# New lists of jobs for the front and the attention of a retention, MLP and attention kernel; two chunks' scores in wider blocks; the last chunk's keys left in HBM

## The chip, the cores and the metric

One core of a Trainium2 chip runs the kernel. The metric is the device time of one execution in microseconds, as the median of repeated runs. Engines are named as the profile names them: PE multiplies matrices (PEld is its loading of weights), DVE, ACT and POOL work on elements, and SP issues most of the DMA transfers.

## The reference

Three layers on 2 batches of 768 positions, all in fp32:

```python
# retention, 8 heads of 64, blocks of 64 positions
intra = einsum(einsum(qb, kb) * Dmask, vb)          # Dmask[i, j] = lam ** (i - j) for i >= j
out   = intra + einsum(qb * lam_pow, kv_state)
kv_state = lam ** block * kv_state + einsum(kb * rev_pow, vb)
# layer norm and MLP, 512 -> 2048 -> 512
x = x + relu(layer_norm(x) * g_ln @ w_ch1) @ w_ch2
# four experts, each a causal softmax attention with 64 columns; the two best by x @ w_gate are mixed
```

## The kernel before

**Retention.** Each batch is cut into 6 chunks of 128 positions, 12 in all. For chunk n, `load_qk` brings queries and keys with the head's columns on the partitions, and `load_kv` keys and values with the positions on the partitions; each is one transfer of 512 KB. Then, with the letters of the list: `S` scores on PE into PSUM (`ret_scores`), `A` their decay on DVE, `Ka` and `Kg` the keys' scaling for the state (three heads on ACT, five on POOL), `Q` the queries' scaling on POOL, `T` the chunk's state on PE, `D` the running state on DVE, `O` its decay on POOL, `U` queries by state on PE, `I` decayed scores by values on PE, on top of `U`, and `C` three copies of the result out of PSUM on ACT. The last chunk of a batch, numbers 5 and 11, needs no `T`, and so no `Ka` or `Kg`. `S` and `U` with `I` write tiles of two PSUM banks, of which there are two ("big"); four tiles of one bank ("mid") serve the others.

**Layer norm and MLP.** Three chunks make a block of 384 positions. `ma`, `mc`, `mm`, `mi` are the sums, their copy on ACT, the mean on PE and its subtraction on DVE; `sq`, `va`, `vc`, `vd` do the same for the variance; `xs` and `lo` split the block into two parts in fp32r. A weight piece comes as raw words and is unpacked by `z` and `h` on ACT and `l`, `t`, `r`, `e`, `p` on DVE. `P` is one MLP step on PE, twelve matmuls of 384 columns, and `LA`, `LD` are its ReLU on ACT and DVE. 

**Order of the front.** All engines work through one list written out by hand, `FRONT`. Every token is issued in that order on its engine, and each engine takes its own instructions in order. `k`, `q` and `w` issue the loads of kv, qk and weights on the SP queue, `G` the load of the norm's gain on ACT's queue, `W` three warm-up matmuls. Two tokens of different engines that wait for nothing of each other are free against each other.

**Attention.** After the MLP, projections of a block of positions are 8 jobs (`f` takes the next: three of values, the gate, four of queries and keys). Rows of 128 queries with an expert each are items 0 to 47, in the order of `ROWS`. `s` are scores on PE with mask, maximum and exponential behind them, `c` the weighting on POOL, `t` the transposes on PE, `v` weights by values, `o` the output. `ORDER` sets PE's order and the order in which the other engines' work is written; for those the scheduler chooses. The weights before their transpose have 7 buffers, those after it 8.

Of the kernel before, what the change touches and what calls it, by code (L numbers as in the profile page):

```python
# [71 lines left out]

# [3 lines left out]


FRONT = """
    Ka:0 S:0 Kg:0 k:1 S:1 T:0 q:2 A:0 Ka:1 G D:0 A:1 I:0 k:2 W w Kg:1 q:3 O:0 T:1 S:2 C:0 Q:1 D:1 q:4 Q:2 U:1 Ka:2
    w z:0 k:3 I:1 Kg:2 k:4 S:3 O:1 A:2 Q:4 l:0 t:0 q:5 U:2 T:2 C:1 I:2 A:3 h:0 Q:3 q:6 k:5 D:2 S:4 Kg:3 q:7 C:2  # L80
    O:2 Ka:3 A:4 U:3 r:0 T:3 e:0 Kg:4 D:3 z:1 I:3 k:6 C:3 l:1 O:3 w Ka:4 ma:0 q:8 p:0 S:5 mc:0 k:7 Ka:6 U:4 mm:0
    I:4 A:5 T:4 Kg:6 Q:5 D:4 C:4 mi:0:0 sq:0:0 S:6 A:6 T:6 Q:7 U:5 mi:0:1 t:1 xs:0:0 I:5 D:6 xs:0:1 O:6 S:7 I:6
    C:5 xs:0:2 k:8 Kg:7 w lo:0:1 sq:0:1 k:9 Ka:7 va:0 C:6 ma:1 A:7 q:9 T:7 xs:0:3 lo:0:0 S:8 lo:0:2 Kg:8 Q:8
    Ka:8 U:7 D:7 Kg:9 O:7 h:1 lo:0:3 k:10 I:7 A:8 mc:1 r:1 T:8 C:7 Kg:10 q:10 mm:1 mi:1:0 mi:1:1 P:g1:0:0:0 S:9
    Ka:9 xs:1:0 Ka:10 e:1 U:8 D:8 LA:g1:0:0:0 xs:1:1 xs:1:2 I:8 C:8 T:9 q:11 vc:0 sq:1:0 A:9 k:11 w Q:9 O:8
    sq:1:1 Q:11 lo:1:2 z:2 S:10 lo:1:1 lo:1:0 vd:0 A:10 U:9 Q:10 D:9 p:1 I:9 xs:1:3 lo:1:3 va:1 C:9 ma:2 l:2
    S:11 O:9 t:2 U:10 LD:g1:0:0:0 vc:1 I:10 T:10 mc:2 vd:1 mm:2 h:2 P:g1:0:1:0 r:2 D:10 C:10 mi:2:0 P:g1:0:0:1
    xs:2:0 U:11 e:2 mi:2:1 xs:2:1 A:11 LA:g1:0:1:0 lo:2:0 w sq:2:0 LD:g1:0:1:0 xs:2:2 I:11 xs:2:3 sq:2:1 lo:2:3
    P:g1:0:1:1 LA:g1:0:0:1 p:2 LD:g1:0:0:1 C:11 park:0 LA:g1:0:1:1 z:3 va:2 lo:2:2 LD:g1:0:1:1 park:1 ma:3 l:3
    t:3 P:g1:0:0:2 lo:2:1 z:4 X mc:3 LA:g1:0:0:2 h:3 vc:2 r:3 mm:3 mi:3:0 e:3 mi:3:1 xs:3:0 p:3 P:g1:0:1:2  # L90
    xs:3:1 LD:g1:0:0:2 LA:g1:0:1:2 xs:3:2 z:5 LD:g1:0:1:2 P:g1:0:2:0 l:4 P:g1:0:2:1 w LA:g1:0:2:0 l:5 P:g1:0:2:2
    lo:3:2 t:4 sq:3:1 P:g1:0:0:3 lo:3:1 LD:g1:0:2:0 LA:g1:0:2:1 h:4 r:4 P:g1:0:1:3 LA:g1:0:2:2 LD:g1:0:2:1
    sq:3:0 LA:g1:0:0:3 xs:3:3 park:2 park:3 t:5 LD:g1:0:2:2 va:3 vc:3 h:5 P:g1:0:2:3 e:4 lo:3:3 p:4 P:g2f:0:0:0
    w LD:g1:0:0:3 LA:g1:0:1:3 z:6 lo:3:0 r:5 LA:g1:0:2:3 LD:g1:0:1:3 P:g1:0:3:0 w l:6 e:5 p:5 P:g2f:0:0:1 t:6 w
    h:6 LD:g1:0:2:3 z:7 r:6 P:g1:0:3:1 l:7 LA:g1:0:3:0 e:6 LA:g1:0:3:1 vd:3 LD:g1:0:3:0 w p:6 vd:2 t:7 h:7
    LD:g1:0:3:1 r:7 e:7 p:7
"""


# [950 lines left out]
```

## Time and profile before

| what | value |
|---|---|
| median of 3 runs | 457.24 us (457.09 to 457.62) |
| the profiled execution | 457.37 us, its span 455.6 us |
| granted TensorE clock | 1.00 in every stage |
| busy share of the span: PE, DVE, ACT, POOL | 98%, 73%, 46%, 18% |
| front, attention | 0 to 98 us, 322.4 to 455.6 us |

The span runs from the first to the last instruction. The profiled execution's own time is longer by what lies around its instructions. Ends of matmuls are modelled, so PE counts as busy over short waits; the distance between starts tells them.

### The profile page before, as it was taken

How to read it: one execution, taken by the hardware profiler on the slowest of the kernel's cores; microseconds unless marked ns; L12 is line 12 of the kernel's file. 1: busy time of each engine (PE TensorE's matmuls, PEld its weight loads, DVE VectorE, ACT ScalarE, POOL GpSimd, SP SyncE). 2: the span in 40 equal slices, each digit the busy share in tenths (PEclk: the TensorE clock that was granted, in tenths of full speed). 3: DMA queues.
4: the chain of work that ended last, by engine and by line, in shares of the span. 5: the costliest groups of instructions: out<-in, count | busy, mean ns of one | idle time of the engine just before them, and what ended most of it. 6: DMA issues, size and time to landing. Idle time of an engine off the chain costs nothing.

```text
span 455.6 us, 9079 instructions
## 1 busy us (share of the span) xinstructions
PE 447.5 (98%) x3563; PEld 421.5 (93%) x3563; DVE 331.9 (73%) x698; ACT 208.9 (46%) x476; POOL 83.2 (18%) x132
## 2 busy tenths in 40 slices
...
GB/s 295 393 371 288 137 83 199 93 51 157 122 92 75 65 94 85 54 0 48 90 96 108 182 48 74 36 88 1 0 1 0 25 25 23 24 2 48 24 47 71
DMA packets 15226, 42.33 MB, mean 93 GB/s; under 512 B 2240, under 2 KB 5072, under 8 KB 15184
## 3 DMA queue, kind: packets, MB, share of 16 engines
...
q8 instruction: 28, 0.46, 0.4%
q10 hardware_dynamic: 288, 0.13, 0.1%
...
## 4 chain that ended last, share of the span: by engine, by line
PE 94%; DMA 3%; ACT 1%; issue 0%; POOL 0%; DVE 0%; SPq 0%
PE h L553 29%; PE y L589 27%; PE pj L815 7%; PE s L895 5%; PE av L945 5%; PE t L933 4%; PE pv L837 4%; PE o L966 4%; DMA early<-in_qkT 2%; PE po L431 2%; PE yf L611 2%; PE sc L367 2%; PE ps L412 1%; PE po L422 1%; DMA qk<-in_qkT 1%; PE va L471 1%
## 5 line engine op out<-in xcount | busy, mean ns | idle before, releaser
L553 PE MATMUL h<-xn,w 128*128 128x384 f32 x768 | 139.6, 336 | 0.0
L553 PEld LDWEIGHTS h<-xn,w 128*128 128x128 f32 x768 | 133.5, 188 | 2.2 <-DVE hs L575 0.6
L589 PE MATMUL y<-hs,w 128*128 128x384 f32 x552 | 99.7, 334 | 0.0
L589 PEld LDWEIGHTS y<-hs,w 128*128 128x128 f32 x552 | 96.1, 188 | 0.0
L572 ACT ACTIVATE hs<-h 128x384 fp32r<-128x384 f32 x50 | 24.5, 491 | 114.2 <-PE h L553 104.7
L829 POOL TENSOR_SCALAR kh<-kh 64x384 fp32r<-64x384 f32 x16 | 8.1, 507 | 295.4 <-ACT kh L826 293.4
L575 DVE SCALAR_TENSOR_TENSOR hs<-h,hs 128x384 fp32r<-128x384 f32 x50 | 27.7, 555 | 34.1 <-ACT hs L572 34.1
L923 POOL TENSOR_SCALAR att<-att,c,gw 128x128 f32<-128x128 f32 (+5 forms) x48 | 34.7, 730 | 46.0 <-DVE c L920 24.4
L597 DVE TENSOR_TENSOR xT<-xT,y 128x768 f32<-128x768 f32 x24 | 22.8, 952 | 27.3 <-PE y L589 27.3
L815 PE MATMUL pj<-x,wa 128*128 128x384 f32 x192 | 36.0, 340 | 0.0
L277 ACT CAST w<-top 128x512 fp32r<-128x512 f32 x32 | 19.8, 620 | 30.0 <-DVE top L269 30.0
L815 PEld LDWEIGHTS pj<-x,wa 128*128 128x128 f32 x192 | 33.1, 188 | 0.3 <-issue 0.2
L934 ACT COPY aT<-t 128x512 f32<-128x512 f32 (+3 forms) x64 | 26.4, 442 | 9.2 <-PE t L933 9.0
L933 PE MATMUL t<-ident,att 128*128 128x128 f32 x168 | 26.1, 275 | 0.0
L933 PEld LDWEIGHTS t<-ident,att 128*128 128x128 f32 x168 | 20.1, 140 | 3.1 <-issue 1.2
L895 PE MATMUL s<-kh,qs 128*128 128x384 f32 (+4 forms) x64 | 22.8, 362 | 0.0
L260 ACT ACTIVATE mag<-raw 128x512 f32<-128x512 f32 x31 | 20.4, 670 | 4.6 <-DVE w L288 2.1
L288 DVE TENSOR_TENSOR w<-top,mag 128x512 fp32r<-128x512 f32 x32 | 22.0, 688 | 0.3
L285 DVE TENSOR_TENSOR top<-top,w 128x512 f32<-128x512 f32 x32 | 21.9, 684 | 0.0
L282 DVE SCALAR_TENSOR_TENSOR mag<-raw,mag 128x512 f32<-128x512 uint32 x31 | 21.4, 689 | 0.7
L269 DVE SCALAR_TENSOR_TENSOR top<-raw,mag 128x512 int32<-128x512 int32 x31 | 21.4, 689 | 0.6
L945 PE MATMUL av<-aT,v 128*64 128x128 f32 x336 | 21.5, 277 | 0.0
...
## 6 DMA issues: line engine op xcount, KB each, us to landing
...
```

Of the source, the lines that this page charges most:

```text
L288: nc.vector.tensor_tensor(t["w"][:, 1], t["top"], t["mag"], ALU.add)
L553: nc.tensor.matmul(ph[:, :TB], w[:, wi, k, :], xn[:, xi, k, :], start=(i == 0), stop=(i == 11))
L572: LAST.append([nc.scalar.activation(h[:, 0], ph[:, :TB], AF.Relu)])
L575: LAST[-1].append(nc.vector.scalar_tensor_tensor(h[:, 1], ph[:, :TB], 0.0, h[:, 0].bitcast(F32), ALU.max, ALU.subtract))
L589: nc.tensor.matmul(y[:, j, :TB], w[:, wi, e * P:(e + 1) * P], h[:, xi], start=(f == 0 and i == 0), stop=(f == GF - 1 and i == 2))
L597: nc.vector.tensor_tensor(xv, xv, y[:, :, :TB], ALU.add)
L815: nc.tensor.matmul(ps[:, :TB], w[:, wi, k, :], x2[:, xi, k, :], start=(i == 0), stop=(i == 11))
L895: nc.tensor.matmul(ps[:, c], q, kk[:, e, c * m:(c + 1) * m], start=(i == 0), stop=(i == 1))
L923: nc.gpsimd.tensor_scalar(a[:, :n], a[:, :n], c, gw, ALU.mult, ALU.mult)
L933: nc.tensor.transpose(pt[:, (j - j0) * P:(j - j0 + 1) * P], a[:, j * P:(j + 1) * P], ident)
L934: nc.scalar.copy(aT[:, j0 * P:j1 * P], pt[:, :(j1 - j0) * P])
L945: nc.tensor.matmul(pav[e2 * HD:(e2 + 1) * HD, pr * P:(pr + 1) * P], v[:, j, e * HD:(e + 1) * HD], row["aT"][e][:, j * P:(j + 1) * P], star ...
```

## The change

`FRONT` and `ORDER` hold the same tokens in another order. In `ret_scores` the first two chunks take one matmul per head with 128 stationary columns instead of two with 64. For the last chunk of a batch `load_kv` brings the values alone.

```diff
+WHOLE = 2
 ORDER = """
-    s0 s1 f f s2 s3 c0 s4 c1 c2 s5 c3 f s6 c4 s7 t0 t1 f c5 f t2 c6 f t3 s8 c7 s9 t4 c8 s10 v1 v3 t5 c9 c10 f t6
...
-    f s19 t13 f t14 f f o11 c18 f t15 s20 c19 s21 t16 s22 c20 t17 v13 v15 s23 t18 s24 f o15 s25 c21 t19 c22 c23
...
-    s31 s32 t27 o23 t28 s33 c30 t29 s34 c31 c32 s35 v25 v27 c33 c34 c35 t30 s36 c36 o27 t31 s37 c37 t32 s38 v29
...
-    t41 s46 v37 v39 c45 t42 c46 s47 t43 v41 v43 t44 t45 o39 c47 t46 t47 v45 v47 o43 o47
+    s0 s1 c0 c1 s4 f s5 f f c5 s2 s3 c4 f s6 c3 c6 s7 t1 t4 f s8 f s9 f t0 c7 f c9 s10 s11 f t7 s12 f t3 t5 f v1 t8
+    t2 s16 c2 c11 s13 v3 v5 t6 o3 c13 v7 t10 f s17 t11 s18 f s19 f s14 c19 t9 f c18 c17 s15 f c12 c15 f s20 s21 t17
+    t13 f v9 v11 t19 t18 c16 c14 s24 f s22 f t14 c20 s23 c10 c23 f f t16 f c21 c8 t12 t15 s25 o11 s26 c24 f t22 s28
+    v13 v15 v17 s27 t23 t20 s29 t21 o15 s30 c25 v21 v19 t25 s31 c27 s32 t27 s33 c26 c29 o19 c22 t29 c28 c31 s34 t28
+    s35 s36 v23 t24 o7 s37 t26 c33 c35 t34 v25 s38 t31 s40 c36 t32 c30 v29 v27 s41 t36 c38 s42 t35 c41 t30 s43 t33
+    o23 s39 v31 v33 v35 t38 c43 o31 t40 c37 o27 t37 t41 s44 c39 t39 s45 c44 v41 v37 c34 v39 c45 t42 s46 s47 t44 c32
+    c47 c42 t43 c46 t45 o39 o35 t46 t47 v43 v45 c40 v47 o43 o47
 """
 FRONT = """
-    Ka:0 S:0 Kg:0 k:1 S:1 T:0 q:2 A:0 Ka:1 G D:0 A:1 I:0 k:2 W w Kg:1 q:3 O:0 T:1 S:2 C:0 Q:1 D:1 q:4 Q:2 U:1 Ka:2
-    w z:0 k:3 I:1 Kg:2 k:4 S:3 O:1 A:2 Q:4 l:0 t:0 q:5 U:2 T:2 C:1 I:2 A:3 h:0 Q:3 q:6 k:5 D:2 S:4 Kg:3 q:7 C:2
-    O:2 Ka:3 A:4 U:3 r:0 T:3 e:0 Kg:4 D:3 z:1 I:3 k:6 C:3 l:1 O:3 w Ka:4 ma:0 q:8 p:0 S:5 mc:0 k:7 Ka:6 U:4 mm:0
-    I:4 A:5 T:4 Kg:6 Q:5 D:4 C:4 mi:0:0 sq:0:0 S:6 A:6 T:6 Q:7 U:5 mi:0:1 t:1 xs:0:0 I:5 D:6 xs:0:1 O:6 S:7 I:6
...
-    sq:1:1 Q:11 lo:1:2 z:2 S:10 lo:1:1 lo:1:0 vd:0 A:10 U:9 Q:10 D:9 p:1 I:9 xs:1:3 lo:1:3 va:1 C:9 ma:2 l:2
-    S:11 O:9 t:2 U:10 LD:g1:0:0:0 vc:1 I:10 T:10 mc:2 vd:1 mm:2 h:2 P:g1:0:1:0 r:2 D:10 C:10 mi:2:0 P:g1:0:0:1
...
+    k:1 Kg:0 Ka:0 S:0 A:0 G W Q:1 k:2 Kg:1 q:2 S:1 Kg:2 T:0 D:0 O:0 I:0 Ka:1 U:1 q:3 Q:2 q:4 T:1 Ka:2 T:2 A:1 I:1
+    S:2 D:1 O:1 D:2 w k:3 C:0 w k:4 S:3 U:2 Q:4 Q:3 q:5 A:2 I:2 k:5 S:4 Kg:3 C:1 O:2 C:2 ma:0 k:6 q:6 A:3 z:0 Ka:3
+    q:7 l:0 T:3 D:3 t:0 O:3 Kg:4 Kg:6 mc:0 Ka:4 h:0 A:4 q:8 r:0 z:1 U:3 I:3 mm:0 T:4 l:1 S:5 k:7 U:4 A:5 mi:0:0 Q:5
+    I:4 Q:7 D:4 t:1 C:3 C:4 k:8 Ka:6 S:6 A:6 U:5 I:5 q:9 q:10 T:6 e:0 sq:0:0 k:9 S:7 mi:0:1 xs:0:0 D:6 I:6 C:5 ma:1
...
+    xs:1:1 A:9 T:9 xs:1:2 sq:1:0 C:8 sq:1:1 lo:1:2 e:1 p:1 O:8 k:11 Q:9 q:11 Q:11 P:g1:0:0:0 LA:g1:0:0:0 z:2 vc:0
+    vd:0 lo:1:1 lo:1:0 xs:1:3 S:10 D:9 O:9 U:9 I:9 z:3 A:10 ma:2 Ka:10 lo:1:3 va:1 mc:2 l:2 mm:2 mi:2:0 C:9 vc:1
+    T:10 Q:10 xs:2:0 mi:2:1 xs:2:1 D:10 l:3 t:2 h:2 LD:g1:0:0:0 r:2 U:10 S:11 t:3 vd:1 A:11 I:10 C:10 P:g1:0:1:0
...
 """
@@ def load_kv
-        nc.sync.dma_start(kvn, kv[b, c])
+        if c < NC - 1:
+            nc.sync.dma_start(kvn, kv[b, c])
+        else:
+            nc.sync.dma_start(kvn[:, 1], kv[b, c, :, 1])
@@ def ret_scores
         for hp, h2 in HEADS:
+            if n < WHOLE:
+                nc.tensor.matmul(sc[:, h2, cols(hp)], r["qk"][half(h2), 1, hp, :], r["qk"][half(h2), 0, hp, :],
+                                 start=True, stop=True, skip_group_check=True)
+                continue
             for kh in range(2):
```

## Rows read from the trace of the kernel before

**Rows 1.** The page: busy time, share of the span and instructions of each engine.
```profile
PE 447.5 (98%) x3563; PEld 421.5 (93%) x3563; DVE 331.9 (73%) x698; ACT 208.9 (46%) x476; POOL 83.2 (18%) x132
```
**Rows 2.** Windows: stretch, busy PE, PEld, DVE, ACT, POOL; clock; DMA share, GB/s.
```profile
16.20:28.00 11.80, 11.15 (x252) 8.64 (x252) 7.98 (x11) 5.50 (x17) 5.56 (x7) 1.00 1.02 408
28.00:39.50 11.50, 11.26 (x245) 8.54 (x243) 10.57 (x15) 10.49 (x29) 8.95 (x10) 1.00 0.97 358
39.50:57.20 17.70, 17.70 (x284) 14.80 (x282) 16.14 (x26) 14.73 (x34) 6.11 (x6) 1.00 0.48 165
...
98.00:322.40 224.40, 224.40 (x1296) 224.40 (x1295) 158.66 (x272) 68.05 (x120) 0.00 (x0) 1.00 0.25 77
322.40:455.60 133.20, 129.91 (x1047) 119.64 (x1046) 97.67 (x301) 82.50 (x223) 51.76 (x80) 1.00 0.07 25
```
**Rows 3.** The chain that ended last: start, us, what.
```profile
28.06 1.03 PE sc L367 x32
...
45.02 1.03 PE sc L367 x32
...
57.22 0.60 PE po L422 x16
...
65.48 12.48 PE h L553 x72
```
**Rows 4.** Timeline of PE from 16 us: start, us, instruction, count, idle before.
```profile
16.21 1.10 PE L367 MATMUL sc<-early 64*64 64x128 f32 x32 [2.01 <-DMA early<-in_qkT]
17.11 0.65 PE L422 MATMUL po<-qd,st 64*64 64x128 f32 x16
17.68 0.69 PE L412 MATMUL ps<-kvn,kd 128*64 128x64 f32 x16
18.20 1.05 PE L431 MATMUL po<-a,kvn 128*64 128x128 f32 x16
19.17 1.10 PE L367 MATMUL sc<-qk 64*64 64x128 f32 x32
```
**Rows 5.** Groups by line and shape, 5 to 57 us: busy us, mean ns; idle before.
```profile
L398 DVE TENSOR_TENSOR a<-sc,dec 128x1024 f32<-128x1024 f32 x12 | 14.6, 1220 | 4.1 <-PE sc L367 4.1
...
L457 ACT COPY xT<-po 64x256 f32<-64x256 f32 x22 | 8.1, 367 | 0.3
...
L392 POOL TENSOR_TENSOR kd<-kvn,dec 128x320 f32<-128x320 f32 x8 | 6.7, 836 | 5.5 <-PE po L431 2.9 <-DVE a L398 1.1 <-PE ps L412 1.0
...
L441 DVE TENSOR_TENSOR st<-ps,old 128x256 f32<-128x256 f32 x8 | 3.4, 419 | 2.8 <-PE ps L412 2.8
...
L392 POOL TENSOR_TENSOR kd<-early,dec 128x320 f32<-128x320 f32 x2 | 1.5, 730 | 0.0
```
**Rows 6.** Timeline of ACT and its queue, 9 to 14 us.
```profile
9.19 0.38 ACTq L688 DMA_DIRECT2D g_sb<-in_g_ln  x1
...
11.81 0.83 ACT L386 ACTIVATE kd<-kvn,dec 128x64 f32<-128x64 f32 x3 [0.29 <-DMA kvn<-in_kv]
13.13 0.71 ACT L260 ACTIVATE mag<-raw 128x512 f32<-128x512 f32 x1 [0.49 <-DMA raw<-in_w]
```
**Rows 7.** Timeline of all engines around 381 us.
```profile
380.25 0.47 ACT L826 CAST kh<-pj 64x384 fp32r<-64x384 f32 x1 [1.58 <-PE pj L815]
...
381.65 0.42 PE L895 MATMUL s<-kh,qs 128*128 128x384 f32 x1
...
382.24 0.44 PE L895 MATMUL s<-kl,qs 128*128 128x384 f32 x1 [0.17 <-POOL kl L829]
```
**Rows 8.** Timeline of PE from 444 us.
```profile
444.68 1.97 PE L945 MATMUL av<-aT,v 128*64 128x128 f32 x32
...
448.56 0.92 PE L945 MATMUL av<-aT,v 128*64 128x128 f32 x8
449.40 3.07 PE L966 MATMUL o<-wa,avs 128*128 128x512 f32 x18
```
**Rows 9.** The page: costliest groups, out<-in count, busy us, mean ns, idle before.
```profile
L934 ACT COPY aT<-t 128x512 f32<-128x512 f32 (+3 forms) x64 | 26.4, 442 | 9.2 <-PE t L933 9.0
```

More of the change, by code (lines that the diff above doesn't have):

```diff
@@ L62 @@
 ORDER = """
-    s0 s1 f f s2 s3 c0 s4 c1 c2 s5 c3 f s6 c4 s7 t0 t1 f c5 f t2 c6 f t3 s8 c7 s9 t4 c8 s10 v1 v3 t5 c9 c10 f t6
-    f s11 s12 t7 s13 f t8 c11 o3 f t9 s14 t10 c12 s15 v5 c13 v7 s16 c14 f t11 s17 c15 c16 t12 c17 s18 o7 v9 v11
-    f s19 t13 f t14 f f o11 c18 f t15 s20 c19 s21 t16 s22 c20 t17 v13 v15 s23 t18 s24 f o15 s25 c21 t19 c22 c23
-    s26 t20 c24 f f t21 c25 c26 s27 t22 f c27 f t23 f v17 v19 f f s28 s29 t24 c28 o19 c29 t25 s30 v21 v23 t26
-    s31 s32 t27 o23 t28 s33 c30 t29 s34 c31 c32 s35 v25 v27 c33 c34 c35 t30 s36 c36 o27 t31 s37 c37 t32 s38 v29
-    c38 v31 t33 s39 t34 s40 t35 s41 t36 o31 c39 c40 v33 c41 s42 t37 s43 t38 v35 c42 t39 s44 c43 o35 t40 s45 c44
-    t41 s46 v37 v39 c45 t42 c46 s47 t43 v41 v43 t44 t45 o39 c47 t46 t47 v45 v47 o43 o47
+    s0 s1 c0 c1 s4 f s5 f f c5 s2 s3 c4 f s6 c3 c6 s7 t1 t4 f s8 f s9 f t0 c7 f c9 s10 s11 f t7 s12 f t3 t5 f v1 t8
[5 more added lines that the diff above has]
+    c47 c42 t43 c46 t45 o39 o35 t46 t47 v43 v45 c40 v47 o43 o47
 """
@@ L78 @@
 FRONT = """
-    Ka:0 S:0 Kg:0 k:1 S:1 T:0 q:2 A:0 Ka:1 G D:0 A:1 I:0 k:2 W w Kg:1 q:3 O:0 T:1 S:2 C:0 Q:1 D:1 q:4 Q:2 U:1 Ka:2
-    w z:0 k:3 I:1 Kg:2 k:4 S:3 O:1 A:2 Q:4 l:0 t:0 q:5 U:2 T:2 C:1 I:2 A:3 h:0 Q:3 q:6 k:5 D:2 S:4 Kg:3 q:7 C:2
-    O:2 Ka:3 A:4 U:3 r:0 T:3 e:0 Kg:4 D:3 z:1 I:3 k:6 C:3 l:1 O:3 w Ka:4 ma:0 q:8 p:0 S:5 mc:0 k:7 Ka:6 U:4 mm:0
-    I:4 A:5 T:4 Kg:6 Q:5 D:4 C:4 mi:0:0 sq:0:0 S:6 A:6 T:6 Q:7 U:5 mi:0:1 t:1 xs:0:0 I:5 D:6 xs:0:1 O:6 S:7 I:6
-    C:5 xs:0:2 k:8 Kg:7 w lo:0:1 sq:0:1 k:9 Ka:7 va:0 C:6 ma:1 A:7 q:9 T:7 xs:0:3 lo:0:0 S:8 lo:0:2 Kg:8 Q:8
@@ L84 @@
-    Ka:8 U:7 D:7 Kg:9 O:7 h:1 lo:0:3 k:10 I:7 A:8 mc:1 r:1 T:8 C:7 Kg:10 q:10 mm:1 mi:1:0 mi:1:1 P:g1:0:0:0 S:9
-    Ka:9 xs:1:0 Ka:10 e:1 U:8 D:8 LA:g1:0:0:0 xs:1:1 xs:1:2 I:8 C:8 T:9 q:11 vc:0 sq:1:0 A:9 k:11 w Q:9 O:8
-    sq:1:1 Q:11 lo:1:2 z:2 S:10 lo:1:1 lo:1:0 vd:0 A:10 U:9 Q:10 D:9 p:1 I:9 xs:1:3 lo:1:3 va:1 C:9 ma:2 l:2
-    S:11 O:9 t:2 U:10 LD:g1:0:0:0 vc:1 I:10 T:10 mc:2 vd:1 mm:2 h:2 P:g1:0:1:0 r:2 D:10 C:10 mi:2:0 P:g1:0:0:1
-    xs:2:0 U:11 e:2 mi:2:1 xs:2:1 A:11 LA:g1:0:1:0 lo:2:0 w sq:2:0 LD:g1:0:1:0 xs:2:2 I:11 xs:2:3 sq:2:1 lo:2:3
@@ L89 @@
[L89 to L93, printed above, removed]
@@ L94 @@
-    w LD:g1:0:0:3 LA:g1:0:1:3 z:6 lo:3:0 r:5 LA:g1:0:2:3 LD:g1:0:1:3 P:g1:0:3:0 w l:6 e:5 p:5 P:g2f:0:0:1 t:6 w
-    h:6 LD:g1:0:2:3 z:7 r:6 P:g1:0:3:1 l:7 LA:g1:0:3:0 e:6 LA:g1:0:3:1 vd:3 LD:g1:0:3:0 w p:6 vd:2 t:7 h:7
-    LD:g1:0:3:1 r:7 e:7 p:7
+    k:1 Kg:0 Ka:0 S:0 A:0 G W Q:1 k:2 Kg:1 q:2 S:1 Kg:2 T:0 D:0 O:0 I:0 Ka:1 U:1 q:3 Q:2 q:4 T:1 Ka:2 T:2 A:1 I:1
+    S:2 D:1 O:1 D:2 w k:3 C:0 w k:4 S:3 U:2 Q:4 Q:3 q:5 A:2 I:2 k:5 S:4 Kg:3 C:1 O:2 C:2 ma:0 k:6 q:6 A:3 z:0 Ka:3
+    q:7 l:0 T:3 D:3 t:0 O:3 Kg:4 Kg:6 mc:0 Ka:4 h:0 A:4 q:8 r:0 z:1 U:3 I:3 mm:0 T:4 l:1 S:5 k:7 U:4 A:5 mi:0:0 Q:5
@@ new lines @@
+    I:4 Q:7 D:4 t:1 C:3 C:4 k:8 Ka:6 S:6 A:6 U:5 I:5 q:9 q:10 T:6 e:0 sq:0:0 k:9 S:7 mi:0:1 xs:0:0 D:6 I:6 C:5 ma:1
+    xs:0:1 Q:8 xs:0:2 O:6 lo:0:1 sq:0:1 va:0 mc:1 Ka:7 w Kg:7 T:7 p:0 A:7 C:6 k:10 xs:0:3 lo:0:0 lo:0:2 Kg:8 Kg:9
+    lo:0:3 mm:1 mi:1:0 S:8 A:8 Ka:8 U:7 D:7 T:8 I:7 C:7 h:1 O:7 Ka:9 r:1 w w D:8 Kg:10 S:9 U:8 I:8 mi:1:1 xs:1:0
+    xs:1:1 A:9 T:9 xs:1:2 sq:1:0 C:8 sq:1:1 lo:1:2 e:1 p:1 O:8 k:11 Q:9 q:11 Q:11 P:g1:0:0:0 LA:g1:0:0:0 z:2 vc:0
+    vd:0 lo:1:1 lo:1:0 xs:1:3 S:10 D:9 O:9 U:9 I:9 z:3 A:10 ma:2 Ka:10 lo:1:3 va:1 mc:2 l:2 mm:2 mi:2:0 C:9 vc:1
@@ new lines @@
+    T:10 Q:10 xs:2:0 mi:2:1 xs:2:1 D:10 l:3 t:2 h:2 LD:g1:0:0:0 r:2 U:10 S:11 t:3 vd:1 A:11 I:10 C:10 P:g1:0:1:0
+    P:g1:0:0:1 LA:g1:0:1:0 lo:2:0 U:11 h:3 LA:g1:0:0:1 r:3 sq:2:0 xs:2:2 xs:2:3 e:2 I:11 sq:2:1 LD:g1:0:1:0 lo:2:3
+    P:g1:0:1:1 LD:g1:0:0:1 p:2 park:0 C:11 e:3 z:4 LA:g1:0:1:1 p:3 LD:g1:0:1:1 va:2 lo:2:2 lo:2:1 l:4 ma:3
+    P:g1:0:0:2 w park:1 X mc:3 mm:3 P:g1:0:1:2 LA:g1:0:0:2 w mi:3:0 mi:3:1 xs:3:0 xs:3:1 LA:g1:0:1:2 vc:2 P:g1:0:2:0
+    LA:g1:0:2:0 LD:g1:0:0:2 P:g1:0:2:1 t:4 h:4 xs:3:2 z:5 P:g1:0:2:2 P:g1:0:0:3 LA:g1:0:2:1 LA:g1:0:2:2 lo:3:2
```

4 lines of the change are left out of this document (added).

## The prediction

> **What bounds the kernel now.** I read the page's engine line first, then the granted clock and the busy times stage by stage, then the chain of waits, then the timeline of single engines where the chain is not plain PE work. PE is busy 98% of the span [rows 1], so only time in which PE has nothing to do, or waits with a matmul still in its pipe, can be won; the work itself is the same in both versions but for two chunks' scores. The stages [rows 2] say where to look: the clock is 1.00 everywhere; from 98 to 322.4 us PE and its weight loads fill the stage completely and neither list touches the order there. What is left is the front (up to 98 us) and the attention (322.4 us on).
>
> A "busy" PE hides waits, because the modelled end of a matmul covers short ones. So I price a job by the distance between starts [rows 4]: a chunk's scores S 0.90 (16.21 to 17.11), its outer part U 0.57 (to 17.68), its state T 0.52 (to 18.20), its inner part I 0.97 (to 19.17). A layer-norm sum I put at 0.7 and a mean at 0.4 (estimates, from the I and the twelve matmuls of an MLP step, which take 2.08: 12.48 for 72 from 65.48 on [rows 3]).
>
> Front: from the first S at 5.50 to S6 (scores of chunk 6, 28.06 in the chain [rows 3]) PE does 6 S, 5 T, 4 U, 5 I, one sum, one mean and the second warm-up: about 17.0 us of work in 22.6, so 5.5 idle. The largest piece is S3, which waits 2.01 us for its query/key load [rows 4]. Loads come every 1.3 us: two that follow each other release ACT at 11.81 and 13.13 [rows 6]; but the next one comes only at 16.2, 3.1 us later. What the trace has beside them is the gain vector's load, issued at 9.19 [rows 6], in elements of four bytes. I put the missing 1.8 us (3.1 less 1.3) on it. After 28 us loads are no longer last: DVE is busy 10.57 and ACT 10.49 of 11.50, then 16.14 and 14.73 of 17.70 [rows 2]. There PE follows the decay products on DVE and the copies out of PSUM on ACT. From 65.5 to 98 PE runs without a gap, so what is won before stays won.
>
> Attention: 133.2 us [rows 2]. Its plain idle time is small: one score matmul waits for POOL's copy of a key at 382.24, its start 0.59 after its partner's at 381.65 instead of some 0.2 [rows 7] (a score of that width is one pass of 384 columns, 0.17 in an MLP step); with what hangs on it I count 0.6 us. At the end 8 value matmuls take 0.92 where 32 of them take 1.97 [rows 8], so 0.4 of it is waiting, and the last 18 output matmuls take 3.07, of which I put 0.25 on a wait for the copy that they read: 0.65 us together. Some 0.6 more is spread in pieces of about 0.1. So at most 1.9 us can be won here.
>
> **The change, part by part.** *Scores in halves of 64x128, chunks 0 and 1:* 8 matmul calls a chunk instead of 16. No row shows this shape. Nearest below: U's 16 instructions in 0.57; above: I's 16 in 0.97 run two at a time, so twice that, 1.94, if the two row halves did not overlap. A stationary block twice as wide, two at a time, does the same work as four narrow ones, so I take 0.90, no change. What hides 1.0 us a chunk, if it is needed: T0 waits for chunk 0's keys and POOL's scaling until about 8.35 in both lists, and S3 for its load; of 2.0 us at most 0.4 gets through.
>
> *The last chunk's keys are not loaded:* two loads of 512 KB become 256 KB, 0.65 us each by the 1.3 of a full one. They were never used (chunks 5 and 11 have no T). Loads behind chunk 5's come 0.65 earlier. Price: 0 as long as DVE and ACT end the waits, which after 28 us they do [rows 2]; 0.65 if S6 were load-bound.
>
> *The front's list.* Both lists hold the same jobs. I walked the new one engine by engine: a job starts when its engine is free and its last input is there (0.25 us from the last PE start-slot to DVE or ACT), with the prices of [rows 4]: decay A 1.2, state sum D 0.42, three copies C 1.1 (three of 0.37), POOL's key scaling 0.84 or a little less [rows 5], three key scalings on ACT 0.83, the first part of a weight piece 0.7 [rows 6].
> - S3's load is now seventh instead of eighth (the weights' load moves behind it), the gain vector's load is issued 1.2 us earlier but still lies ahead of it: 16.2 - 1.3 = 14.9. S3 runs 14.95 to 15.9, S4 after A3 at 17.4.
> - The next last input is C2 on ACT (18.9), so the first sum waits 0.5; then the first weight piece, whose load is now two places later and whose unpacking on ACT stands behind C2, holds the third chunk's scaling until 20.4 (T3 waits 0.4). T4 waits for POOL at 22.6, S5 for A4 at 23.1, U4 for C3 at 24.3. S6 needs A5, 26.4. Against 28.06: 1.6 us won, with the same PE jobs done.
> - U5 waits for D4, which stands behind A5 and a mean subtraction on DVE (27.7); S7 29.7, S8 34.3, and the first MLP step with chunk 9's state done at 43.0. In the trace the same set is done at 45.0: 1.9 won.
> - Then a new wait. The third mean now stands ahead of T10, U10, S11 and I10. It needs the copy of its sums on ACT, and that is queued behind two squarings, a step's ReLU, two weight pieces and chunk 10's scalings: about 48.2, while PE comes to it at 46.8. Behind it PE's next six jobs wait, 1.4 us. In the old list the mean was last of these and cost nothing.
> - U11 comes at about 56.0 against 57.22 [rows 3]: 1.2 won. By then DVE has 1.4 us more of weight unpacking to do after S6 than in the old list (two parts of the first piece slip behind it), and had only 2.5 us idle between 28 and 57.2 [rows 2]; so I take 1.0 rather than 1.2.
>
> POOL's key scaling has two rows: 730 ns where it reads the separate early tile, 836 on average for the eight others [rows 5]; the eight cost 0.9 us more than the short one would. I read that as time lost beside DVE, and take it as it stands. [...]
>
> Bounds for the front: 3 us won if the new wait does not come and DVE keeps pace; 1 us lost if DVE and ACT fall behind by what they had idle.
>
> *The attention's list.* I counted PE work between dependent jobs, by the list. From a projection of keys to the first score that reads it: least distance 1.7 us in the old list, 6.9 in the new. The trace needs 2.0 (ACT begins to copy the keys at 380.25, the waiting matmul starts at 382.24 [rows 7]). So the 0.6 us goes. At the end two value matmuls of another row now stand between the last transposes and the matmuls that read them (1.2 us of PE work instead of 0.25), so the 0.4 goes too; the output matmul that follows needs only the first ACT copy, 0.5 us after, and has 0.46 of cover. From the last scores to their transposes there are 3.4 us of PE work instead of 3.9; the trace's chain of mask, maximum, exponentials and weighting takes 3.2, so it just fits. Sum won: 0.6 + 0.4 + about 0.2 = 1.2. Against it: the new list runs scores so far ahead that up to 10 rows of weights are alive in 7 buffers (8 at most before). An exponential then waits for a transpose, and its PSUM pair with it. For three score jobs (rows of batch 1, near 411 to 418 us) the distance from that transpose is only 1.1, 1.4 and 1.6 us, where an exponential with the copy before it takes 0.7 to 1.7: 0 to 1.5 us, I take 0.3. Net 0.9 won; bounds 1.9 won, 1.0 lost.
>
> Sum: 1.0 + 0.9 = 1.9 us off a span of 455.6. The profiled execution took 457.37, 1.8 around its span, and is 0.13 above the median 457.24; nothing in the change touches what lies around it. 457.24 - 1.9 = 455.3.
>
> **Rivals.** *1. ACT and DVE set the front's pace (within 0.2%).* For it: 10.57 and 10.49 of 11.50 [rows 2]; a PE that arrives earlier only waits longer. POOL's stretched scalings [rows 5] would add up to 0.9 us where PE waits for them. Against it: 3.8 us of DVE idle before 28 us. Front 0, attention 0.9 less slips: 456.6 to 457.2.
> *2. The seven buffers decide (slower).* Place: the 22 score jobs of the new list that begin with more than 7 rows of weights alive (one in the old). Mechanism: the scheduler, not the list, orders ACT; where it puts the copy of a transpose ahead of the exponential that the transpose frees, PE's next score job waits for its PSUM pair by one such copy, 0.44 us on average [rows 9]. It decides from 5 jobs on (2.2 us, all that is won before the 0.3); with 8 of the 22 it costs 3.5: 457.24 - 2.2 + 3.5 = 458.5. Against it: away from the three jobs above, the distance from the transpose to the job that needs the pair is 2.3 us or more.
> *3. More is won.* The third mean's copy comes in time, since ACT ran with 3 us of slack in 39.5 to 57.2 [rows 2], and attention loses nothing at its buffers: 2.2 + 1.5: 453.5.
> *4. The key loads do nothing:* that is part of the forecast, not a case apart.
>
> **How the numbers follow.** A measurement of this kernel tells from no change about 0.2%, 0.9 us. Forecast (454.3 to 456.3) 0.43; rival 3 (about 453.5) 0.15; rival 1 0.21; rival 2 0.21. Faster by over 0.2% is the forecast, rival 3 and a little of rival 1: 0.60; within 0.2% 0.20; slower 0.20. The likeliest one's own range is 454.3 to 456.3; the range reaches to 453.0 (front and attention near their bounds) and 458.0, which leaves out some part of rivals 2 and 3, about 1 in 10 on either side.
>
> **What the new profile would show.** S3 ends its wait near 15 us and S6 starts near 26.4; the third mean has a wait for ACT; U11 near 56; the y/h stretch to 322 unbroken but about 1 us earlier; no wait for POOL's key copy in the attention; the last value matmuls without a gap. I am wrong if S6 starts near 28 again (then ACT or DVE ends it), if the score jobs in the attention wait for ACT, or if a wait appears before an MLP step between 65 and 98 us, where DVE's last weight pieces come just in time.

## The result and the profile after

The changed kernel takes 463.04 us (462.91 to 463.45, 4 runs) where the kernel before took 457.43 on the same chip: ratio 1.0121, interval 1.0103 to 1.0138. It is slower by 5.6 us; the forecast was 455.3, with slower at 0.20. Letters and numbers of steps are those of the list, so S6 is the scores of chunk 6 (the seventh), A5 the decay of chunk 5 (the sixth). Lines of the changed kernel are 3 to 7 higher than before.

Windows of the changed kernel by stage, columns as in [rows 2]: front, MLP, attention.

```profile
4.00:102.80 98.80, 92.52 (x1183) 77.31 (x1182) 78.41 (x125) 56.00 (x131) 29.83 (x36) 0.98 0.60 212
102.80:327.70 224.90, 224.90 (x1298) 224.90 (x1297) 158.45 (x272) 68.24 (x120) 0.00 (x0) 1.00 0.24 77
327.70:461.70 134.00, 130.53 (x1047) 119.85 (x1046) 93.44 (x301) 81.51 (x223) 51.72 (x80) 1.00 0.07 25
```

The front ends at 102.8 and not 97.5: 5.3 us lost. MLP as before; attention 134.0 against 133.2 [rows 2]: 0.8 lost.

What PE waited for from 5 to 70 us (operation, releaser, us, times, longest):

```profile
PE sc L374 <- DVE a L405: 2.4, 2, 2.2
PE po L429 <- issue: 1.0, 1, 1.0
PE po L429 <- DVE a L405: 0.9, 1, 0.9
PE mean L487 <- ACT mus L483: 0.7, 1, 0.7
PE sc L370 <- DMA qk<-in_qkT: 0.4, 1, 0.4
```

The 2.0 us for a load [rows 4] is gone; three others stand there. The PE timeline of the changed kernel shows two of them in place, U2 and S6:

```profile
15.08 1.10 PE L374 MATMUL sc<-early 64*64 64x128 f32 x32 [0.20 <-ACT xT L464]
16.32 0.66 PE L429 MATMUL po<-qd,st 64*64 64x128 f32 x15
18.00 0.32 PE L429 MATMUL po<-qd,st 64*64 64x128 f32 x1 [1.01 <-issue]
18.25 0.33 PE L438 MATMUL po<-a,kvn 128*64 128x128 f32 x2
...
26.96 1.09 PE L438 MATMUL po<-a,kvn 128*64 128x128 f32 x16
30.23 1.10 PE L374 MATMUL sc<-qk 64*64 64x128 f32 x32 [2.18 <-DVE a L405]
```

S3 starts at 15.08, 1.1 us earlier than in [rows 4]. But U2 stops before its last matmul for 1.3 us (16.71 to 18.00) with no semaphore to wait for, and S6, which PE could have begun at 28.0, waits for A5 until 30.23 ([rows 3]: 28.06). U11 then starts at 62.24, 5.0 us after [rows 3].

Why A5 was late is in the timeline of DVE in the changed kernel (idle before in brackets):

```profile
21.29 0.43 DVE L267 TENSOR_SCALAR mag<-mag 128x512 f32<-128x512 f32 x1 [3.81 <-ACT mag L263]
...
23.53 1.22 DVE L405 TENSOR_TENSOR a<-sc,dec 128x1024 f32<-128x1024 f32 x1
24.67 0.42 DVE L284 TENSOR_SCALAR mag<-top 128x512 int32<-128x512 int32 x1
25.12 1.10 DVE L285 SCALAR_TENSOR_TENSOR mag<-raw,mag 128x512 f32<-128x512 uint32 x1
26.14 1.49 DVE L267 TENSOR_SCALAR mag<-mag 128x512 f32<-128x512 f32 x1
27.67 1.38 DVE L268 TENSOR_SCALAR mag<-mag 128x512 int32<-128x512 int32 x1
28.97 1.21 DVE L405 TENSOR_TENSOR a<-sc,dec 128x1024 f32<-128x1024 f32 x1
```

POOL (GpSimd) in the same timeline:

```profile
25.64 1.72 POOL L382 TENSOR_TENSOR qd<-qk,qpow 128x512 f32<-128x512 f32 x1
27.32 1.45 POOL L382 TENSOR_TENSOR qd<-early,qpow 128x512 f32<-128x512 f32 x1
```

DVE stands idle for 3.8 us up to 21.29, since the first weight piece is taken up late (z0 stands behind C2 on ACT). Then r0 (L284, L285) and l1 (L267, L268) lie in front of A5, and the same L267 and L268 that take 0.43 us at 21 us take 1.49 and 1.38 beside GpSimd's products. Each ends 0.3 us behind the product that it overlaps (27.64 behind 27.35, 29.05 behind 28.77).

Windows of the changed kernel around S6, columns as in [rows 2]:

```profile
20.00:28.00 8.00, 7.89 (x154) 5.40 (x146) 6.19 (x9) 5.22 (x15) 5.91 (x7) 1.00 0.98 366
28.00:35.00 7.00, 4.63 (x80) 4.04 (x80) 7.00 (x8) 3.66 (x10) 2.03 (x2) 0.76 0.66 238
```

The second of these windows in e2 below, which has the same front's list:

```profile
28.00:35.00 7.00, 4.63 (x120) 3.94 (x120) 7.00 (x9) 4.95 (x12) 2.06 (x2) 1.00 0.78 262
```

Behind the idle time PE worked at a granted clock below full speed (0.50 from 31.5 to 34.9 us and 1.00 ahead of that and behind it, 0.76 over the window); in e2's profiled execution, after the same wait, it did not. The two stand level at S6 (30.23 and 30.25). U11 of the changed kernel, then of e2:

```profile
62.24 0.67 PE L429 MATMUL po<-qd,st 64*64 64x128 f32 x16
60.71 0.67 PE L429 MATMUL po<-qd,st 64*64 64x128 f32 x16
```

So of the 5.0 us at U11, 2.2 were there at S6, 1.5 went with the clock, and 1.3 were lost behind S6 at full clock.

### The profile page after: what moved, and what is told of

Read it like the earlier page. It is cut to its first block, busy times and chain, and to the rows that moved or that the text cites. A ratio compares the mean times of both kernels' runs of the same rounds, so it can differ in the third digit from the quotient of the medians.

```text
span 461.7 us, 8993 instructions
## 1 busy us (share of the span) xinstructions
PE 450.8 (98%) x3531; PEld 423.1 (92%) x3531; DVE 330.9 (72%) x698; ACT 207.2 (45%) x476; POOL 84.2 (18%) x132
## 4 chain that ended last, share of the span: by engine, by line
PE 91%; ACT 3%; DMA 2%; DVE 2%; issue 1%; SPq 0%; POOL 0%; ACTq 0%; POOLq 0%
PE h L560 29%; PE y L596 27%; PE pj L822 6%; PE s L902 5%; PE av L952 4%; PE t L940 4%; PE pv L844 4%; PE o L973 4%; PE po L438 2%; PE yf L618 2%; DMA kvn<-in_kv 1%; PE ps L419 1%; PE po L429 1%; DMA early<-in_kv 1%; PE sc L374 1%
## 5 line engine op out<-in xcount | busy, mean ns | idle before, releaser
L280 ACT CAST w<-top 128x512 fp32r<-128x512 f32 x32 | 19.8, 620 | 29.6 <-DVE top L272 29.6
L940 PE MATMUL t<-ident,att 128*128 128x128 f32 x168 | 24.9, 277 | 0.0
L285 DVE SCALAR_TENSOR_TENSOR mag<-raw,mag 128x512 f32<-128x512 uint32 x31 | 22.1, 713 | 0.6
L272 DVE SCALAR_TENSOR_TENSOR top<-raw,mag 128x512 int32<-128x512 int32 x31 | 21.3, 689 | 0.5
```

Source lines behind the costliest of these rows:

```text
L940: nc.tensor.transpose(pt[:, (j - j0) * P:(j - j0 + 1) * P], a[:, j * P:(j + 1) * P], ident)
```

## The experiments

All ratios are to the kernel before on the same chip, with 95% intervals.

| run | edit | us | ratio |
|---|---|---|---|
| e1 | before, new attention list | 457.95 | 1.0014 (1.0005 to 1.0024) |
| e2 | changed, old attention list | 462.08 | 1.0099 (1.0079 to 1.0118) |
| e3 | before, whole scores, short loads | 457.36 | 1.0000 (0.9990 to 1.0009) |
| e4 | changed, l1 behind A5 | 461.75 | 1.0103 (1.0072 to 1.0135) |
| e5 | changed, z0, l0, t0 early | 461.33 | 1.0080 (1.0054 to 1.0106) |
| e7 | e5, r0 and A4 early too | 459.97 | 1.0058 (1.0043 to 1.0073) |
| e6 | changed, Kg4 and Q5 early | 460.32 | 1.0065 (1.0050 to 1.0080) |
| e8 | changed, WHOLE = 4 | 459.75 | 1.0067 (1.0042 to 1.0092) |
| e9 | before, new order of loads | 457.41 | 1.0006 (0.9996 to 1.0015) |
| e10 | e9, D2 early | 458.18 | 1.0029 (1.0018 to 1.0039) |
| e11 | changed, all mended, old attention list | 457.36 | 0.9998 (0.9989 to 1.0007) |
| e12 | e11 to S6, then the old list | 456.81 | 0.9994 (0.9984 to 1.0004) |
| e13 | e12, A6 ahead | 455.94 | 0.9976 (0.9965 to 0.9987) |

**Which list, which part: e1, e2, e3.** e1 is the kernel before with the new `ORDER`, e2 the changed one with the old `ORDER`, e3 the kernel before with these lines alone:

```diff
+WHOLE = 2
+        if c < NC - 1:
+            nc.sync.dma_start(kvn, kv[b, c])
+        else:
+            nc.sync.dma_start(kvn[:, 1], kv[b, c, :, 1])
```

> The kernel before with the new list of the attention alone. In the changed kernel the attention took 134.0 us against 133.2 before. Theory A (the new list of the attention itself loses that): front end and MLP as before, first y stretch at 97.5 us, time 458.2 us (457.8 to 458.6). Theory B (the list is neutral, and the 0.8 us came with what the front left over): 457.4 us (457.2 to 457.7). If the forecast's 0.9 us of gain is in it and the front hid it: 456.5 us.

> The changed kernel with the old list of the attention: the front's list, the whole scores and the short loads stay. Theory A: the front carries 5.3 us of the loss and the attention's list 0.8, so 462.2 us (461.8 to 462.7), first y stretch still at 102.9 us. Theory B (the attention's list is neutral): 463.0 us.

> The kernel before with both of its old lists, and only the two small parts of the change: the scores of chunks 0 and 1 whole, and the last chunk of a batch loaded without its keys. Theory A (as the forecast priced them): the whole scores at 0.05 to 0.2 us a chunk more, hidden ahead of the wait at the fourth chunk's scores; the short load lands 0.6 us earlier and hides: 457.2 us (456.9 to 457.6). Theory B (the fetch of instructions comes at another place since 64 are missing, and TensorE stands for it): 458 to 459 us.

The attention's list alone costs 0.7 us, not the 0.9 won that was forecast; the two small parts cost nothing in the time (e3; what they moved inside is told at e8 and e9). The rest, some 4.7 us from e3 to e2, is the front's list. Of e2's four executions two ran at a mean granted clock of 0.999 (461.33 and 461.42 us) and two at 0.996 (462.74 and 462.87): the clock is worth 1.4 us there, and all runs of the changed kernel were at 0.995 or 0.996. At 0.999 e2 lies 4.0 us above e3. Most executions of e4, e5 and e8, and all of e6 and e7, were at 0.999 or 1.00, so what their medians win on the changed kernel holds some of the clock too. U11 tells it apart: the profiled executions of e2, e6, e7, e8 and e11 were all at full clock up to there.

**The late decay: e4, e5, e7.**

```diff
 # e4
-mm:0 T:4 l:1 S:5 k:7 U:4 A:5 mi:0:0 Q:5
+mm:0 T:4 S:5 k:7 U:4 A:5 l:1 mi:0:0 Q:5
 # e5, against the changed kernel
-O:2 C:2 ma:0 k:6 q:6 A:3 z:0 Ka:3 q:7 l:0 T:3 D:3 t:0 O:3
+O:2 z:0 C:2 ma:0 k:6 q:6 A:3 Ka:3 q:7 l:0 t:0 T:3 D:3 O:3
 # e7, against e5
-q:7 l:0 t:0 T:3 D:3 O:3 Kg:4 Kg:6 mc:0 Ka:4 h:0 A:4 q:8 r:0 z:1
+q:7 l:0 t:0 r:0 A:4 T:3 D:3 O:3 Kg:4 Kg:6 mc:0 Ka:4 h:0 q:8 z:1
```

> The changed kernel with one step of the front's list moved: the clamp of the second weight piece (L267 and L268 on VectorE, 2.9 us there beside GpSimd) goes behind the sixth chunk's decay multiply (L405) that it stood ahead of. Theory A (VectorE reached that decay late, and TensorE's 2.2 us wait at the seventh chunk's scores and the stretch of granted clock 0.66 behind it follow from it): the decay ends at 27.7 us and not 30.2, no wait at those scores, granted clock 1.00 from 30 to 35 us, 2.2 us of wait and some 1.8 us of slow clock won, 459.5 us (458.7 to 460.5). Theory B (VectorE is full up to 70 us whatever the order, so the 1.7 to 2.9 us come back at the next thing that waits for it): the wait moves, time 462 to 463 us. Theory C (the slow clock comes from earlier idling, at 16.7 to 18.0 us, and not from the 2.2 us): the wait goes and the clock from 30 to 35 us stays at 0.66, 461 us.

> The changed kernel with the first weight piece's first three unpacking steps moved up in the list: the magnitude (L263, ScalarE) ahead of the third chunk's copy, clamp and top (L267, L268, L272, VectorE) right behind the fourth decay, into the 3.8 us in which VectorE stood idle. Theory A (the loss is that this idle time was not used and its work came in the way later): VectorE gets 1.5 to 2.5 us of work done in the gap, the sixth decay ends at 27.8 to 29 us and not 30.2, time 461 us (459.5 to 462). Theory B (VectorE's delay is the stretching beside GpSimd alone, and the early steps only move where it happens): 462.5 to 463.5 us. Theory C (TensorE's own 1.25 us stall at 16.7 us and the order of its jobs set the pace): 463 us.

> The changed kernel with the first piece's steps early as in the run before, its remainder (L284, L285) and the fifth decay (L405) ahead of the fourth state's sum too, which VectorE waited for until 22.2 us. VectorE then stands idle for under 1.5 us between 16 and 26 us. Theory A (VectorE's order is what the front lost): the sixth decay ends at 27.6 to 28.0 us, TensorE has no wait over 0.5 us at the seventh chunk's scores and none over 1 us to 45 us, first y stretch at 99 to 100.5 us, time 459.3 us (458.5 to 460.5). Theory B (VectorE's load to 70 us sets the pace, so that order does not matter): 461 to 462.5 us.

e4 came between its two theories, nearer to B: S6 no longer waits, but the next job does, for the state that DVE's sum D4 makes (1.6 us of PE's waits there). Its clock was 1.00 in three of four executions (the fourth, at 0.996, took 464.48); two of e2's four were at 0.999 with the wait still there, so this settles nothing on theory C. e5 came near its theory A in time, by another way than it said: A5 ended at 29.6, hardly earlier, since DVE took the early steps and then waited 3.2 us for D3, behind which A4 stood. With r0 and A4 ahead of D3 (e7) A5 ends at 28.2, and 3.1 us of the 5.6 are back; at the same clock U11 starts at 58.82, 1.9 before e2's. So DVE's order is a part of what held PE up. In e7 DVE is busy for all of 28 to 35 us, and PE's longest waits to 70 us are 0.9 for A1 and 0.9 for GpSimd's keys of chunk 4; which of these keeps the rest was not tried apart.

**GpSimd beside DVE: e6.**

```diff
-T:3 D:3 t:0 O:3 Kg:4 Kg:6 ... A:5 mi:0:0 Q:5
+T:3 D:3 t:0 Kg:4 Q:5 O:3 Kg:6 ... A:5 mi:0:0
```

> The changed kernel with two of GpSimd's products moved up in the list, ahead of the old state's (L454) that GpSimd waited for from 21.0 to 23.1 us: the key product of chunk 4 (L399) and the query product of chunk 5 (L382). The work is the same; less of it stands beside VectorE's unpacking from 24 to 29 us. Theory A (operations of VectorE that read and write SBUF alone take up to 2 to 3.5 times as long beside GpSimd's): L285 falls from 1.10 us to 0.7, L267 and L268 from 1.50 and 1.38 to 0.4 to 1.0, the sixth decay ends 1 to 2 us earlier than 30.2, and the time is 461.5 us (460.5 to 462.5), since a part comes back at the next wait, as in the run with the late clamp. Theory B (these operations are slow there for another reason, the loads for one): they stay at 1.1 to 1.5 us and the time at 462.5 to 463.5.

Theory A, and more of it: 460.32 us, 2.7 less, with all four executions at full clock; U11 starts at 59.48, 1.2 before e2's (1.6 counted from S3, which came 0.4 later in this execution). L267 took 0.94 us and L268 0.43 (1.49 and 1.38 in the changed kernel), A5 ended at 28.97; L285 stayed at 0.99, again beside a product. Groups of e6 from 14 to 70 us (line, shapes, count, busy us, mean ns, idle before):

```profile
L267 DVE TENSOR_SCALAR mag<-mag 128x512 f32<-128x512 f32 x5 | 2.9, 578 | 3.8 <-ACT mag L263 3.8
...
L268 DVE TENSOR_SCALAR mag<-mag 128x512 int32<-128x512 int32 x5 | 2.1, 427 | 0.2
```

The same groups of the changed kernel:

```profile
L267 DVE TENSOR_SCALAR mag<-mag 128x512 f32<-128x512 f32 x5 | 3.2, 635 | 3.8 <-ACT mag L263 3.8
L268 DVE TENSOR_SCALAR mag<-mag 128x512 int32<-128x512 int32 x5 | 3.1, 617 | 0.2
```

Over the whole trace of the changed kernel L267 and L268 ran 62 times with nothing on GpSimd beside them, and none took more than 0.43 us; the two beside its products are the 1.49 and the 1.38. The decays (L405), which read PSUM, take 1.21 to 1.23 us in either case. Two that started ahead of a product kept their time: in e7 an L268 that starts at 17.94, 0.08 us ahead of a product, takes 0.43; in the kernel before, L264 (L267 of the changed one) starts at 23.93, 0.16 ahead of a product, and takes 0.42. The L265 behind it (L268 of the changed one) starts at 24.38 beside that product and takes 0.73: it ends at 25.11, the product at 24.83.

**The stop without a semaphore: e8.**

```diff
-WHOLE = 2
+WHOLE = 4
```

> The changed kernel with the scores of chunks 2 and 3 whole too (WHOLE = 4): 64 fewer instructions of TensorE ahead of the place at 16.7 us where it stood 1.25 us for no semaphore. Theory A (instructions are fetched in parts of 16 KB by queue 8, one of them at 15.4 us, and TensorE had run out of them in the dense stretch of 128 score matmuls and weight loads just before): the stall shrinks below 0.5 us or goes, the fourth chunk's decay starts up to 1 us earlier; the time falls by 0 to 1.2 us, to 462.3 us, as far as VectorE lets it. Theory B (the stall belongs to that product's own operands or to its place): it stays at 1.0 to 1.25 us, and the time at 463 us or above, by 0.1 us a chunk for the whole form.

Theory A, and larger than it said: 3.3 us, a part of it the clock. PE's timeline in e8, S2, S3, U2, I2:

```profile
13.79 1.16 PE L370 MATMUL sc<-qk 64*128 64x128 f32 x16
15.09 1.16 PE L370 MATMUL sc<-early 64*128 64x128 f32 x16
16.37 0.67 PE L429 MATMUL po<-qd,st 64*64 64x128 f32 x16
16.97 1.09 PE L438 MATMUL po<-a,kvn 128*64 128x128 f32 x16
```

The two whole scores take 2.58 us from start to start of what follows, the two in quarters 2.54, so the form itself costs nothing; but U2 runs through, S4 starts at 17.99 and not 19.27, and A5 at 26.74, so S6 waits 1.2 us and not 2.2. In four of five executions the clock stays at 1.00 too (459.67 to 459.79; the fifth, at 0.996, took 462.78, 0.3 less than the changed kernel, also at that clock). Between traces at full clock U11 starts at 58.45, 2.3 before e2's.

In all six traces with WHOLE = 2 and the new front's list PE stops after the same instruction, the 440th matmul or weight load of the span, whatever the time. So it does in e3, with the old list, where that is in T2 and not in U2:

```profile
17.53 0.22 PE L420 MATMUL ps<-kvn,kd 128*64 128x64 f32 x1 [0.76 <-issue]
```

It is the count, then, and not the job (theory B). e3 takes no longer than the kernel before: it has this stop of 1.0 us where S3's wait is 1.6 us shorter (told at e9). A window of the changed kernel from 15.3 to 16.5 us has a transfer of 16 KB on the instructions' queue (packets, MB, share):

```profile
q8 instruction: 1, 0.02, 5.4%
```

Its packet starts at 15.39 and PE goes on at 18.00, 2.6 us later. In the other traces it is 2.4 to 2.5 us; in e7, where the packet starts at 15.12, PE goes on at 17.56, so there it stood 0.75 us instead of 1.28. In e3 it is 2.5 (15.08 to 17.53). In the kernel before the packet starts at 13.69 and the 440th instruction comes only at 17.00, 3.3 us later: the wait for S3's load had covered it. In the changed kernel the stop comes behind a dense stretch, S2 and S3 with 64 matmuls and as many weight loads in 2.54 us (13.78 to 16.32), in which the DMA engines' share is 1.02.

**The loads alone: e9, e10.** The kernel before, with the loads in the new order and the unpacking behind them.

```diff
 # e9
-Ka:0 S:0 Kg:0 ... Ka:1 G D:0 ... W w Kg:1 q:3 O:0
+Ka:0 G S:0 Kg:0 ... Ka:1 D:0 ... W Kg:1 q:3 w O:0
-w z:0 k:3 I:1 ... Q:4 l:0 t:0 q:5 U:2 T:2 C:1 I:2 A:3 h:0 Q:3 q:6 k:5 D:2 S:4 Kg:3 q:7 C:2
+w k:3 I:1 ... Q:4 q:5 U:2 T:2 C:1 z:0 I:2 A:3 l:0 t:0 Q:3 q:6 k:5 D:2 S:4 Kg:3 q:7 C:2 h:0
 # e10
-A:3 l:0 t:0 Q:3 q:6 k:5 D:2 S:4
+A:3 D:2 l:0 t:0 Q:3 q:6 k:5 S:4
```

> The kernel before with the loads' order of the front changed alone: the gain vector first on ScalarE's queue, the first weight piece behind the fourth chunk's queries and keys, and that piece's unpacking steps moved back behind the copies and the decay that they would hold up (L260 behind the second copy, L264 to L269 behind the fourth decay, L277 behind the third copy). Theory A (the load part of the forecast holds by itself): the fourth chunk's scores start at 14.9 to 15.5 us and not 16.2, and 0.6 to 1.2 us of that last to the end: 456.5 us (456.0 to 457.0). Theory B (TensorE's instruction stall takes the place of the wait, as in the changed kernel): scores early, a stall of 1 to 1.3 us behind them, 457.4 us (457.0 to 458.0). Theory C (the later unpacking holds up VectorE as in the changed kernel): the wait comes back behind 25 us, 458 to 460 us.

> The kernel of the loads' order with one more move: the third state's sum (L440 there) ahead of the first piece's clamp and top on VectorE, which had held it up until 20.5 us, so that TensorE waited 1.8 us for it. Theory A (order on VectorE ate what the loads' order won): that wait goes, the seventh chunk's scores start 0.5 to 1.5 us before 27.7 us, and the time is 456.3 us (455.8 to 456.9). Theory B (the loads or TensorE's own work bound the stretch to 28 us anyway): a new wait on a load behind 20 us, scores at 27.5 us, 457.2 us (456.9 to 457.5).

In e9 S3 starts at 14.26, 1.95 us before [rows 4], and nothing of it is left at the end: PE waits 1.8 us for D2, which stands on DVE behind l0 and t0, stretched beside GpSimd (L264 to 1.45 us, L268 to 1.63). The time is theory B's, the mechanism is C's at an earlier place. In e10 the wait for D2 is gone and PE waits 1.1 us for GpSimd and then 1.7 us for chunk 3's keys on ACT, which stand behind h0, which waits for t0 until 21.3. Both its theories were wrong: it got slower by 0.9 us than before. Its profile has a granted clock of 0.83 from 20 to 30 us, but the five of its nine executions at 1.00 took 457.85 to 458.18, so the clock is not the whole of it. Earlier loads won nothing here while the orders of three engines behind them stayed as they are.

e3 also tells what S3 waited for. With the loads in the old order, and the gain vector's in its old place, its S3 starts at 14.61 and not 16.21. The load of S3's queries and keys by the two traces (KB, us from issue to landing), before and e3:

```profile
early<-in_qkT SPq DMA_DIRECT2D x1, 512.0 KB, 10.8
early<-in_qkT SPq DMA_DIRECT2D x1, 512.0 KB, 9.1
```

In the kernel before, 15 of the load's 16 parts land from 14.23 to 14.48 and the last at 16.08; in e3 all land by 14.47. So the 2.0 us of [rows 4] are a wait for one late part. What differs ahead of it is the 16 KB packet of instructions, at 13.69 in the kernel before and at 15.08 in e3, behind the load. That this packet held up the one part fits, but was not tried by itself.

**All mended: e11, e12, e13.** e11 joins e6, e7 and e8, puts A1 ahead of D0 (that is PE's 0.9 us for `po` above, where U1 waits for its PSUM) and takes the old `ORDER`.

> The changed kernel with all that the runs pointed at mended: scores of chunks 0 to 3 whole (no stall for instructions), the first piece's steps and the fifth decay early, GpSimd's two products ahead of the old state, the second decay (L405) ahead of the first state's copy (L446), so that the second product with the state waits 0.9 us less, and the old list of the attention. Theory A (these are the causes, and they add up as far as TensorE is waiting): from 459.75 us with the whole scores, 0.7 less for the attention, about 1 for the decay at 11 us and about 1 for VectorE: 457.0 us (456.3 to 458.0). Theory B (they are the same loss seen at different places, VectorE's load to 70 us being the bound): 458.5 to 459.5 us.

> The mended list up to the seventh chunk's scores (25.9 us there, 28.0 in the kernel before), and from there on the remaining steps of the front in the order of the old list; the old list of the attention. Theory A (what the new list won by 26 us, 2.1 us, was lost again between 26 and 57 us by its own later order, in which VectorE stands at full load and is stretched beside GpSimd; the old order needs 29.2 us for that stretch, the new one 31.0): 455.4 us (454.8 to 456.2). Theory B (the stretch behind 26 us waits for the loads, which come no earlier, so that the 2 us are lost in any order): 456.8 to 457.5 us, with waits on a load or on a key product behind one between 28 and 45 us.

> The run with the old order from the seventh chunk's scores on, with that chunk's decay (L405) ahead of three unpacking steps (L288, L291, L272, the last 1.71 us beside GpSimd) that it stood behind on VectorE: TensorE waited 1.1 us for it. Theory A (VectorE's order there is all that ate the 2.1 us): that wait falls below 0.3 us, the first MLP step starts at 38.0 to 38.5 us, the time is 455.8 us (455.2 to 456.5). Theory B (VectorE's load, 9.8 of 10 us from 20 to 30, only passes the wait on to the next decay or state): another wait of about 1 us by 45 us, 456.5 to 457.2 us.

e11 is at 457.36, as its theory A said: the whole loss is taken back, and S6 starts at 25.86. That it is no better than before, though 2.1 us ahead at S6, comes behind S6: DVE is busy for 9.93 of the 10 us from 40 to 50, and PE takes 31.0 us to U11 instead of 29.2. e12 brought little of that back: its number is theory B's, but PE waits for DVE and for no load (A6 stands behind e0, p0 and t1, 1.1 us). With A6 ahead (e13) more lasts, as its theory A said: 1.26 us in time, of 2.2 at S6. What PE waits for in e13 from 5 to 70 us:

```profile
PE ps L419 <- ACT kd L393: 0.6, 1, 0.6
PE po L438 <- ACT xT L464: 0.2, 1, 0.2
```

```diff
 # e13, against e12: the second list begins behind S:6
-D:4 t:1 C:3 C:4 k:8 Ka:6 S:6 e:0 w p:0 sq:0:0 A:6 T:6
+D:4 C:3 C:4 k:8 Ka:6 S:6 A:6 e:0 w p:0 sq:0:0 t:1 T:6
```

S6 starts at 25.81 and the first MLP step at 38.1, 1.4 us earlier than in the kernel before (39.5, where [rows 2] is cut). e13 beats both kernels: 455.94 us, 1.26 less than the kernel before.

## Why the prediction was wrong

- *S3 at 14.95:* the number is right (15.08), by luck. In the changed kernel the load has landed by 13.06, and S3 waits 0.2 us for a copy on ACT (L464). Most parts of the load came 1.4 us earlier (13.06 for 14.48), as priced for its place among the loads, but the 1.8 us put on the gain vector's load are not shown to be its: in e3, with that load unmoved, S3 starts 1.6 us earlier.
- *S4 at 17.4, S6 at 26.4:* **the step that failed**, and with it the sum's 1.0 us won in the front, which lost 5.3. The walk priced every job at its spacing in the old trace and gave PE its instructions for nothing. S4 came at 19.27, 1.3 of it the stop in U2, and S6 at 30.23, 2.2 of it the wait for A5, which the next two points explain. The stop comes with the old list too once S3's wait is short: 1.0 us in e3.
- *"I read that as time lost beside DVE, and take it as it stands"*, for GpSimd's key scaling: failed. The forecast looked at the stretch on GpSimd (0.9 us) and not on DVE, where one unpacking step grows from 0.43 to 1.4. On DVE the stretch before A5 is 2.4 us (L285 1.10 for 0.69, L267 and L268 2.87 for 0.86), and e6 won 1.2 at U11 (2.7 in the medians, with the clock).
- *A5 behind nothing:* the walk set S6's end by A4 and S5. It did not see that the first piece's steps, moved two loads later, would leave DVE idle for 3.8 us and then stand in A5's way. e7 shows that this and the stretch are worth 1.9 at U11 (3.1 in the medians, with the clock).
- *The third mean, 1.4 us for ACT:* right in kind, 0.7 in size (53.2 to 53.9 us).
- *DVE's 1.4 us more unpacking behind S6, priced at 0.2:* mis-sized. From 28 us on DVE has hardly any idle time to give (7.00 of 7.00 busy to 35 us above), so what was lost ahead of it is not regained: S6 was 2.2 us late, U11 5.0, and 3.5 of that at full clock (e2).
- *The clock:* the forecast had 1.00 throughout. In the changed kernel it falls behind the idle time at S6, which costs 1.4 to 1.5 us. Why it falls in some executions of the same front and not in others stays open.
- *Whole scores at 0, short loads at 0:* right (e3). It was not foreseen what half as many instructions are worth: 2.3 us at U11 in e8.
- *Attention, 0.9 won:* wrong, 0.7 lost (e1). The key copy's wait is gone from PE's waits, as predicted. What came in its place is seen at the weight loads; e1 from 322 us on (releaser, us, times, longest):

```profile
PEld pj L815 <- PE t L933: 0.4, 1, 0.4
PEld s L895 <- ACT att L908: 0.4, 1, 0.4
PEld av L945 <- ACT gw L863: 0.4, 1, 0.4
PEld o L966 <- ACT avs L951: 0.3, 1, 0.3
```

  Each is a short wait of another kind. In the whole of that view the waits that end at a named instruction sum to 2.3 us in e1 and to 1.2 before. The one for the weights `att` fits rival 2 in kind, 0.4 us and not 3.5. Transposes, in 35 groups instead of 45, take some 1.7 us more beyond their own time than before (counted from start to start), scores 0.7 less. Why more time passes around fewer, larger groups of transposes was not tried, and stays open.
- *Rival 1* named a part of the cause, ACT and DVE setting the front's pace with GpSimd's stretch, but put its floor at "no change". The chance of 0.20 for slower stood on rival 2, which is not what made the kernel slower. The range ended at 458.0 because every term's loss was bounded by the waits of the old trace. The gains were taken off a list in which a wait of 2 us covered the stop.

The shares don't add: at U11 and full clock, 2.3 (e8), 1.9 (e7) and 1.2 (e6) are each taken off the same loss; e11, with all of them and A1, starts U11 at 56.83, 3.9 before e2, and is 4.7 below it in the medians.
